# An FFT and token-mixing kernel: both DRAM bounces read back in pieces behind each write, and batch 1's first transform moved behind batch 0's last stage

## The chip, the cores and the metric

One core of a Trainium2 chip. The metric is the device time of one launch in microseconds (us), as the median of several runs. The kernel before took 667.63 us (3 runs, 667.39 to 667.77). PE is the tensor engine, which does the matmuls; ACT, DVE and POOL are the scalar, vector and GpSimd engines. SBUF is the core's own memory of 128 partitions (rows), which DMA, the transfer hardware with its 16 engines, reaches through ports. Each engine works through its instructions in order, and nearly all the transfers discussed here are issued, in order, by one queue (SP). The kernel holds its own scheduler: when it is built, it decides in which order each engine gets its instructions.

## The reference

Eight batches of 3072 rows by 256 columns. First a Fourier mixing layer, then a channel mix over neighbouring tokens:

```python
# x: (8, 3072, 256); w_r, w_i: (256, 256); w_k: (256, 1024); w_v: (1024, 256)
X = np.fft.rfft(x, axis=1)
Yr = X.real @ w_r - X.imag @ w_i + b_r
Yi = X.real @ w_i + X.imag @ w_r + b_i
Y  = shrink(Yr, 0.01) + 1j * shrink(Yi, 0.01)          # sign(v) * max(|v| - 0.01, 0)
y  = np.fft.irfft(Y, n=3072, axis=1)

prev = shift y by one token, zeros first               # (cut: written with np.concatenate)
k = np.maximum((mu_k * y + (1 - mu_k) * prev) @ w_k, 0)
v = (k * k) @ w_v
r = sigmoid((mu_r * y + (1 - mu_r) * prev) @ moe_w_r)
out = r * v
```

## The kernel before

The transform of 3072 points is split into 96 x 32, so a batch goes through three stages of matmuls. Between them, the index that lies on the partitions has to change, and this is done by writing a tile to DRAM and reading it back with the axes exchanged, a "bounce":

- `first` (8 matmul groups, L287): FFT over 96 points. It leaves tile A, 96 partitions, in four quarters of 8 columns each. Bounce A writes each quarter and reads the whole back as A2, 128 partitions.
- `middle` (L344 and on): FFT over 32 points, the layer's weights, and back. It leaves tile V in six pieces u = 0..5. Bounce V writes them and reads the whole back as V2, 96 partitions.
- `last` (8 groups, L489): the inverse over 96 points. Then the channel mix, called the token stage, in six tiles a batch (matmuls at L575, L600 and L617).

All three stages of batch b run beside the tokens of batch b - 1. The parts that the change touches:

```python
    r1_pool, ym_pool, v_pool, v2_pool = pool("r1p", 2), pool("ymp", 3), pool("vp", 3), pool("v2p", 4)
    ...
    READ_US, WRITE_US = 7.0, 5.0          # what the scheduler assumes of a read and of a write

    # first(b), for each quarter q of the columns
                def store(k):
                    nc.sync.dma_start(out=Adr[b][:, 8 * q:8 * q + 8, :], in_=a)          # 96 partitions, 384 KB
                    ...                                                                  # x loads of a later batch
                    if q == 3:
                        at(k + WRITE_US, fetch)

                def fetch(k):
                    A2[b] = a2_pool.tile([128, NG, D], BF16, name="A2")
                    for cj in range(4):                                                  # 4 reads of 32 partitions
                        nc.sync.dma_start(out=A2[b][32 * cj:32 * cj + 32],
                                          in_=Adr[b][24 * cj:24 * cj + 24].rearrange("g n d -> n g d"))
    ...
            needs = [("x", b, q), "FT"] + [("mid", 0)] * (b == 1)    # first(1) may follow middle(0)

    # middle(b), for each piece u
                def store(k):
                    for cj in range(4):                                                  # 4 writes of 32 partitions
                        nc.sync.dma_start(
                            out=Vdr[b][24 * cj + 4 * u:24 * cj + 4 * u + 4].rearrange("g n d -> n g d"),
                            in_=vt[32 * cj:32 * cj + 32])
                    if u == NU - 1:
                        at(k + WRITE_US, fetch)

                def fetch(k):
                    for q in range(4):
                        V2[b, q] = v2_pool.tile([96, 8, D], BF16, name="V2")
                    for q in (2, 3, 0, 1):                                               # 4 reads of 96 partitions
                        nc.sync.dma_start(out=V2[b, q], in_=Vdr[b][:, 8 * q:8 * q + 8, :])

    # the schedule
    START = 60.0
    ... first(b, *((45.0, 52.0) if b == 1 else (s - 0.9 * P, s - 0.1 * P)))
    ... last(b, 55.0, 60.0) if b == 0 else last(b, s + 0.75 * P, s + 0.95 * P)
```

An A read copies runs of 256 elements, 512 bytes, so it moves in packets of 512 bytes. A V2 partition is contiguous in DRAM; the whole-V reads move runs of 4 KB.

## Time and profile before

| | before |
|---|---|
| time | 667.63 us |
| PE idle, from the trace's records of PE | about 60 us, of which 45 before 93 us |
| batch 0: first middle matmul / first matmul of `last` / first token matmul | 31.9 / 76.4 / 85.8 us (each counted from its weight load; the prediction's 87.3 is the first token matmul itself) |
| period in the steady part, from one batch's first `last` matmul to the next's (batches 1 to 6) | 73 to 78 us |

The page's list of transfers (destination <- source, queue, count, size of one, median us from issue to landing) says that each read of the two bounces was a wide 384 KB one:

```profile
A<-Adr SPq DMA_DIRECT2D x32, 384.0 KB, 6.6
V<-Vdr SPq DMA_DIRECT2D x32, 384.0 KB, 6.2
```

### The profile page before, as it was taken

The page shows a single profiled execution, that of the slowest core. Times are in us where ns is not written, and L with a number is a line of the kernel's source. Part 1 is how long each engine was busy: PE and PEld are TensorE (multiplying, and loading weights), DVE is VectorE, ACT ScalarE, POOL GpSimd, SP SyncE. Part 2 cuts the span into 40 slices and gives each one's busy share as a digit, 9 for nine tenths or more (in the row PEclk, how much of TensorE's full clock was granted, in tenths as well). Part 3 has the DMA queues.
Part 4 walks back from the last instruction along what each step waited for, and adds up shares of the span by engine and source line. Part 5 has one row for each costly group of instructions (what it writes and reads, how often), then busy time and mean ns, then how long its engine had stood idle before and what let it go on. Part 6 is the DMA issues. An engine that isn't in the chain of part 4 may idle for free.

```text
span 662.8 us, 12033 instructions
## 1 busy us (share of the span) xinstructions
PE 593.6 (90%) x4722; PEld 435.5 (66%) x4801; DVE 483.8 (73%) x732; ACT 443.5 (67%) x469; POOL 25.2 (4%) x57
## 2 busy tenths in 40 slices
PE   4295379999999989998999989999999999999996
PEld 1273247777776767765777767766777777777764
DVE  5164368788778877797678787688677896788883
ACT  6254357767777767776577767778687767766662
POOL 5021000000000000000000000000000000000000
PEclk9689579999999999999999999999999999999999
DMA  8697996362247954488155874379233852362223
GB/s 182 119 189 166 290 213 121 79 183 65 57 112 175 230 128 111 103 227 197 33 128 128 237 146 96 88 202 207 86 104 104 223 113 68 78 183 56 65 72 88
DMA packets 75593, 90.33 MB, mean 136 GB/s; under 512 B 8976, under 2 KB 59920, under 8 KB 75536
## 3 DMA queue, kind: packets, MB, share of 16 engines
q1 hardware_dynamic: 69696, 75.53, 44.5%
q0 software_dynamic: 5840, 14.03, 12.5%
q8 instruction: 37, 0.61, 0.4%
q14 instruction: 20, 0.16, 0.1%
HBM read 53.22 MB, written 50.33 MB: 156 GB/s over the span
## 4 chain that ended last, share of the span: by engine, by line
PE 66%; DMA 17%; ACT 6%; DVE 5%; issue 3%; SPq 1%; POOL 0%; DVEq 0%; ACTq 0%; POOLq 0%
PE banks L617 22%; PE banks L575 19%; PE banks L394 11%; DMA Adr<-A 7%; DMA A<-Adr 6%; PE banks L600 4%; ACT rl L581 3%; PE banks L361 3%; PE banks L418 2%; PE banks L383 2%; ACT A L234 2%; PE banks L287 2%; DMA Vdr<-V 1%; DVE V L236 1%; PE banks L489 1%
## 5 line engine op out<-in xcount | busy, mean ns | idle before, releaser
L581 ACT ACTIVATE rl<-banks 128x1024 bf16<-128x1024 f32 x192 | 195.0, 1029 | 86.1 <-PE banks L575 73.2
L575 PE MATMUL banks<-xk,wk 128*128 128x512 bf16 x706 | 191.1, 383 | 4.0 <-DVE xk L553 1.4
L617 PE MATMUL banks<-wv,k 128*128 128x256 bf16 x1536 | 184.5, 274 | 0.4 <-DVE k L587 0.3
L587 DVE TENSOR_TENSOR k<-rl 128x1024 bf16<-128x1024 bf16 x192 | 131.8, 687 | 53.6 <-ACT rl L581 53.5
L617 PEld LDWEIGHTS <-k 128*128 128x128 bf16 x1536 | 150.3, 98 | 30.1 <-issue 1.8
L575 PEld LDWEIGHTS <-wk 128*128 128x128 bf16 x768 | 73.4, 98 | 57.9 <-issue 4.3
L394 PEld LDWEIGHTS <-XT 128*128 128x128 bf16 x768 | 75.4, 98 | 23.9 <-issue 0.8
L402 ACT ACTIVATE r<-banks,neglam 128x1024 bf16<-128x1024 f32 x48 | 53.4, 1113 | 40.6 <-PE banks L394 39.4
L406 DVE SCALAR_TENSOR_TENSOR Y<-banks,r 128x1024 bf16<-128x1024 f32 x48 | 58.5, 1222 | 28.1 <-ACT r L402 28.0
L394 PE MATMUL banks<-wr,XT 128*128 128x256 bf16 x384 | 73.8, 274 | 0.9
L394 PE MATMUL banks<-wi,XT 128*128 128x256 bf16 x384 | 73.8, 274 | 0.0
L553 DVE SCALAR_TENSOR_TENSOR xk<-diff,muk,YT 128x512 bf16<-128x512 bf16 x96 | 70.0, 746 | 0.6
L553 DVE SCALAR_TENSOR_TENSOR xr<-diff,mur,YT 128x512 bf16<-128x512 bf16 x96 | 69.2, 745 | 0.0
L624 DVE TENSOR_TENSOR o<-banks,rg 128x1024 f32<-128x1024 f32 x48 | 58.5, 1218 | 7.7 <-PE banks L617 7.7
L234 ACT ACTIVATE XT<-banks 128x1024 bf16<-128x1024 f32 (+2 forms) x39 | 37.8, 970 | 35.4 <-PE banks L361 23.5
L234 ACT ACTIVATE A<-banks 96x1024 bf16<-96x1024 f32 x49 | 49.2, 1020 | 17.6 <-DMA Adr<-A 12.0
L287 PE MATMUL banks<-xs,FT 96*96 96x512 bf16 x128 | 39.5, 420 | 19.0 <-ACT A L234 11.7
L600 PE MATMUL banks<-wrm,xr 128*128 128x256 bf16 x384 | 49.8, 272 | 3.5 <-ACT rl L581 2.2
L234 ACT ACTIVATE YT<-banks 128x768 bf16<-128x768 f32 x51 | 39.9, 815 | 16.2 <-PE banks L489 16.2
L605 ACT ACTIVATE rg<-banks 128x1024 bf16<-128x1024 f32 x48 | 49.2, 1026 | 1.9 <-PE banks L600 1.9
L600 PEld LDWEIGHTS <-xr 128*128 128x128 bf16 x384 | 37.1, 97 | 14.1 <-issue 3.8
L234 ACT ACTIVATE V<-banks 128x1024 bf16<-128x1024 f32 x33 | 33.8, 1023 | 9.9 <-PE banks L418 8.1
(91 smaller groups left out, 401.8 us busy)
## 6 DMA issues: line engine op xcount, KB each, us to landing
out_dram<-o SPq DMA_DIRECT2D x192, 128.0 KB, 2.2
xs<-in_x_dram POOLq DMA_DIRECT2D x32, 384.0 KB, 8.1
Adr<-A SPq DMA_DIRECT2D x32, 384.0 KB, 6.6
A<-Adr SPq DMA_DIRECT2D x32, 384.0 KB, 6.6
Vdr<-V SPq DMA_DIRECT2D x192, 64.0 KB, 1.8
V<-Vdr SPq DMA_DIRECT2D x32, 384.0 KB, 6.2
wk<-in_moe_w_k_dram POOLq DMA_DIRECT2D x1, 512.0 KB, 5.4
wv<-in_moe_w_v_dram POOLq DMA_DIRECT2D x1, 512.0 KB, 8.4
```

What stands on the lines that cost most here:

```text
L234: nc.scalar.activation(out, in_, AF.Copy, bias=0.0, scale=1.0)
L287: nc.tensor.matmul(ps[:96, 512 * i:512 * i + 512], FT, xt[:, 4 * p + 2 * i:4 * p + 2 * i + 2, :], start=True, stop=True)
L394: nc.tensor.matmul(o, lhs, w[:, c, :], start=False, stop=(w is wi and c == NCD - 1 and (i == 1 or not (u or half))))
L402: nc.scalar.activation(r1, ps, AF.Relu, bias=neglam, scale=1.0)
L406: nc.vector.scalar_tensor_tensor(out=y, in0=ps, scalar=LAM, in1=r1, op0=ALU.add, op1=ALU.min)
L553: nc.vector.scalar_tensor_tensor(out=m[:, c, :], in0=df[:, c, :], scalar=mu[:, c:c + 1], in1=yp[:, c, :], op0=ALU.mult, op1=ALU.add)
L575: nc.tensor.matmul(ps[:, 512 * f:512 * f + 512], wk[:, c, 128 * ff:128 * ff + 128], xk[:, c, :], start=(c == 0), stop=(c == NCD - 1))
L581: nc.scalar.activation(rl, ps, AF.Relu, bias=0.0, scale=1.0)
L587: nc.vector.tensor_tensor(out=k2, in0=rl, in1=rl, op=ALU.mult)
L600: nc.tensor.matmul(ps[:, 256 * q:256 * q + 256], xr[:, c, 128 * q:128 * q + 128], wrm[:, c, :], start=(c == 0), stop=(c == NCD - 1))
L617: nc.tensor.matmul(ps[:, 256 * q:256 * q + 256], K2[t][:, ff, 128 * q:128 * q + 128], wv[:, ff, :], start=(ff == 0), stop=(ff == NCF - 1))
L624: nc.vector.tensor_tensor(out=o.rearrange("p q d -> p (q d)"), in0=ps, in1=rg, op=ALU.mult)
```

## The change

Its intent: a read need not wait for the whole write. When a quarter of A, or a piece of V, has landed in DRAM, that part is read back at once, so that the read of the whole is nearly done when the last part is written. And batch 0's `last` stage no longer stands behind batch 1's `first`, so that tokens can begin earlier. Cut to its core:

```diff
-    ... v2_pool = ... pool("v2p", 4)
+    ... v2_pool = ... pool("v2p", 1)
-    READ_US, WRITE_US = 7.0, 5.0
+    READ_US, WRITE_US = 4.0, 4.0
@@ first(b), quarter q
+                    at(k + WRITE_US, fetch)
+
+                def fetch(k):
+                    if q == 0:
+                        A2[b] = a2_pool.tile([128, NG, D], BF16, name="A2")
+                    for cj in range(4):
+                        p0 = 32 * cj + 8 * q
+                        nc.sync.dma_start(out=A2[b][p0:p0 + 8],
+                                          in_=Adr[b][24 * cj:24 * cj + 24, 8 * q:8 * q + 8].rearrange("g n d -> n g d"))
                     if q == 3:
-                        at(k + WRITE_US, fetch)
-                def fetch(k):
-                    A2[b] = a2_pool.tile([128, NG, D], BF16, name="A2")
-                    for cj in range(4):
-                        nc.sync.dma_start(out=A2[b][32 * cj:32 * cj + 32],
-                                          in_=Adr[b][24 * cj:24 * cj + 24].rearrange("g n d -> n g d"))
-            needs = [("x", b, q), "FT"] + [("mid", 0)] * (b == 1)
-            if q == 3 and p == 1 and b >= 2:
+            needs = [("x", b, q), "FT"] + [("last", 0)] * (b == 1)
+            if q == 0 and p == 0 and b >= 2:
                 needs.append(("mid", b - 2))
@@ middle(b), piece u
+                    at(k + WRITE_US, fetch)
+
+                def fetch(k):
+                    if u == 0:
+                        V2[b] = v2_pool.tile([96, N2, D], BF16, name="V2")
+                    for cj in range(4):
+                        r0 = 24 * cj + 4 * u
+                        nc.sync.dma_start(out=V2[b][r0:r0 + 4], in_=Vdr[b][r0:r0 + 4])
-                    if u == NU - 1:
-                        at(k + WRITE_US, fetch)
-                def fetch(k):
-                    for q in range(4):
-                        V2[b, q] = v2_pool.tile([96, 8, D], BF16, name="V2")
-                    for q in (2, 3, 0, 1):
-                        nc.sync.dma_start(out=V2[b, q], in_=Vdr[b][:, 8 * q:8 * q + 8, :])
@@ (cut: the first use of the one V2 buffer waits for the last stage of the batch before)
@@ schedule
-    START = 60.0
+    START = 50.0
+            fc += last(b, 45.0, 50.0)                                            # b == 0
+            fb += first(b, START, START + 1.0) if b == 1 else first(b, s - 0.9 * P, s - 0.2 * P)
@@ (cut: the scheduler's assumed times for x, FT and the tables, by a few us)
```

So A is read in 16 pieces of 8 partitions, 96 KB each, and V in 24 pieces of 4 partitions, 64 KB each.

More of the change, by code (lines that the diff above doesn't have):

```diff
@@ L57 @@
     a_pool, a2_pool, xt_pool, xt0_pool = pool("ap", 3), pool("a2p", 2), pool("xtp", 3), pool("xt0p", 1)
-    r1_pool, ym_pool, v_pool, v2_pool = pool("r1p", 2), pool("ymp", 3), pool("vp", 3), pool("v2p", 4)
+    r1_pool, ym_pool, v_pool, v2_pool = pool("r1p", 2), pool("ymp", 3), pool("vp", 3), pool("v2p", 1)
     yt_pool, mx_pool, rl_pool, k2_pool = pool("ytp", 2), pool("mxp", 2), pool("rlp", 3), pool("k2p", 2)
@@ L211 @@
     heap, seq = [], itertools.count()
-    free = {"pe": 0.0, "act": 8.0, "dve": 14.0}
+    free = {"pe": 0.0, "act": 6.0, "dve": 13.3}
     done, slots = {}, {}
@@ L303, in store @@
                         done["x", n // 4, n % 4] = k + 9.0
-                    if q == 3:
-                        at(k + WRITE_US, fetch)
-                def fetch(k):
-                    A2[b] = a2_pool.tile([128, NG, D], BF16, name="A2")
-                    for cj in range(4):
-                        nc.sync.dma_start(out=A2[b][32 * cj:32 * cj + 32],
-                                          in_=Adr[b][24 * cj:24 * cj + 24].rearrange("g n d -> n g d"))
-                    done["A2", b] = k + READ_US
-                    if b == 0:
+                    at(k + WRITE_US, fetch)
[6 more added lines that the diff above has]
+                                          in_=Adr[b][24 * cj:24 * cj + 24, 8 * q:8 * q + 8].rearrange("g n d -> n g d"))
+                    if q == 3:
+                        done["A2", b] = k + READ_US
+                    if b == 0 and q == 3:
                         nc.gpsimd.tensor_copy(out=junk, in_=A2[0][:, 0, 0:1])
@@ L318, in fetch @@
                             load_x(1, n)
-                            done["x", 1, n] = k + 18.0
+                            done["x", 1, n] = k + 20.0
                 at(end, evac)
-            needs = [("x", b, q), "FT"] + [("mid", 0)] * (b == 1)
-            if q == 3 and p == 1 and b >= 2:
+            needs = [("x", b, q), "FT"] + [("last", 0)] * (b == 1)
+            if q == 0 and p == 0 and b >= 2:
                 needs.append(("mid", b - 2))
@@ L434, in store @@
                     done["v", b, u] = k + WRITE_US
-                    if u == NU - 1:
-                        at(k + WRITE_US, fetch)
-                def fetch(k):
-                    for q in range(4):
-                        V2[b, q] = v2_pool.tile([96, 8, D], BF16, name="V2")
-                    for q in (2, 3, 0, 1):
-                        nc.sync.dma_start(out=V2[b, q], in_=Vdr[b][:, 8 * q:8 * q + 8, :])
-                    done["V2", b] = k + READ_US
+                    at(k + WRITE_US, fetch)
[5 more added lines that the diff above has]
+                        nc.sync.dma_start(out=V2[b][r0:r0 + 4], in_=Vdr[b][r0:r0 + 4])
+                    if u == NU - 1:
+                        done["V2", b] = k + READ_US
                 if u == NU - 1:
@@ L464, in middle @@
                 needs = [("y", b, u), "GI"]
-                if u == NU - 1 and b >= 1:
+                if u == 0 and b >= 1:
                     needs.append(("last", b - 1))
@@ L488, in issue @@
                     for c in range(NCD):
-                        nc.tensor.matmul(pv[:, c, :, i, :], V2[b, n2 // 8][:, n2 % 8, 128 * c:128 * c + 128],
+                        nc.tensor.matmul(pv[:, c, :, i, :], V2[b][:, n2, 128 * c:128 * c + 128],
                                          FI, start=True, stop=True)
@@ L680 @@
         s = START + P * (b - 1)
-        fb += first(b, 0.0, 1.0) if b == 0 else first(b, *((45.0, 52.0) if b == 1 else (s - 0.9 * P, s - 0.1 * P)))
-        fa += middle(b, 20.0, 44.0) if b == 0 else middle(b, s, s + 0.5 * P)
-        fc += last(b, 55.0, 60.0) if b == 0 else last(b, s + 0.75 * P, s + 0.95 * P)
+        if b == 0:
+            fb += first(b, 0.0, 1.0)
+            fa += middle(b, 20.0, 44.0)
+            fc += last(b, 45.0, 50.0)
+        else:
+            fb += first(b, START, START + 1.0) if b == 1 else first(b, s - 0.9 * P, s - 0.2 * P)
+            fa += middle(b, s + (0.2 * P if b == 1 else 0.0), s + 0.5 * P)
+            fc += last(b, s + 0.75 * P, s + 0.95 * P)
     for t in range(NT):
@@ L700 @@
     for q in range(4):
-        done["x", 0, q] = 5.0 + 3.3 * q
-    done["FT"] = 8.0
-    at(13.3, tables)
+        done["x", 0, q] = 6.0 + 2.8 * q
+    done["FT"] = 5.0
+    at(16.0, tables)
     tab = [Unit(18.0, 0.1, ["FT"], table_fi)]
@@ L706 @@
     streams = [tok, val, fa, fb, fc, tab]
-    at(60.0 - 7.0, lambda k: mix_tokens(0, k))
+    at(START - 7.0, lambda k: mix_tokens(0, k))
     place, held, t = [0] * len(streams), {}, 0.0
```

## The prediction

> **What bounds the kernel now.** I read the page first (busy shares, slices, groups), then the chain of work that ended last, cut to 55 to 100 us, then the waits of PE, then the DMA view in short windows, because the change is about DMA.
>
> The page's busy line and slices, with the busy tenths of PE in 40 slices of 16.6 us:
>
> ```profile
> PE 593.6 (90%) x4722; PEld 435.5 (66%) x4801; DVE 483.8 (73%) x732; ACT 443.5 (67%) x469; POOL 25.2 (4%) x57
> PE   4295379999999989998999989999999999999996
> DMA  8697996362247954488155874379233852362223
> ```
>
> There are two regimes. From the seventh slice on PE is full, and DMA is about half used. Before that, about 93 us pass with PE half idle. The waits of PE say what the idle time is (columns: waited us, times, longest):
>
> ```profile
> PE banks L344 <- DMA A<-Adr: 23.5, 5, 12.4
> PE banks L287 <- ACT A L234: 11.7, 1, 11.7
> PE banks L287 <- DMA xs<-in_x_dram: 7.0, 2, 6.0
> PE banks L489 <- DMA V<-Vdr: 3.6, 4, 1.6
> ```
>
> L344 is the first matmul of the middle stage, which waits for the whole A bounce to be read back. 12.4 us of it belong to batch 0 at 19.5 to 32 us, 3.4 to batch 1 and the rest to later batches: in the window from 93 us on, the same wait is 7.7 us in 3 times, so the steady stage loses little. The chain shows the second stretch:
>
> ```profile
> 60.30 11.49 DMA Adr<-A
> 71.91 1.23 DVE A L236
> 73.20 8.43 DMA Adr<-A
> 83.54 8.54 DMA A<-Adr
> 93.37 1.71 PE banks L575 x4
> ```
>
> Batch 1's first transform stands on PE and on the DMA queue ahead of batch 0's last stage. Its A writes and the four x loads for later batches hold the DMA engines from 58 to 72 us, batch 0's V is asked for only at 71.2 us, and the token stage starts in earnest at 93 us.
>
> **What the Trainium skill says.** (1) DMA: Bandwidth & Descriptors, section "Why a DMA increments its semaphore by 16 and not by 1": a DMA runs on k engines, k being the largest number up to 16 that divides the slowest dimension of both access patterns, and on this queue the lowest-numbered k. The kernel before has 32 or 96 partitions outermost everywhere, so k is 16. The change makes it 8 for A reads (8 partitions by 24 by 256) and 4 for V reads (4 by 8192). No run so far shows a small k.
> (2) SBUF — State Buffer, section "Door 1: The DMA port swizzle": partitions 0..3 are one port (27.6 GB/s measured), 0..31 eight ports (189 GB/s measured). The trace before agrees. While only A reads into 32 partitions run, the DMA view gives, in 28.4 to 30.2 us,
>
> ```profile
> DMA packets 628, 0.32 MB, mean 177 GB/s; under 512 B 7, under 2 KB 628, under 8 KB 628
> q1 hardware_dynamic: 628, 0.32, 120.8%
> ```
>
> that is 22 GB/s per port. It is no limit of the engines: where V writes to DRAM were queued up (51 to 51.6 us) the same 512 B packets ran at
>
> ```profile
> DMA packets 428, 0.20 MB, mean 329 GB/s; under 512 B 50, under 2 KB 427, under 8 KB 428
> ```
>
> and in 26.6 to 27.4 us, where the reads pass from partitions 32..63 to 64..95, the mean rises to 211 GB/s and falls back.
> (3) Same page, section "Can I just issue two DMAs to hit both halves?": two such DMAs on different partitions gained 6%, as they follow each other on the same engines. Here there is one counter-example: eight out stores of 32 partitions, piled up behind an A read, ran at 402 GB/s at 236 to 237 us, so engines that are out of step can use different ports.
>
> **The change part by part.**
> *Order at the start.* last(0) is put directly behind middle(0), first(1) behind it. PE's order agrees: the 24 matmuls of L287 between the last L418 and the first L489 of batch 0 are gone. It removes the DMA stretch 60 to 84 us from the path of batch 0. If reads were as fast as hoped, tokens would begin about 7 us after V has landed (before: last piece 79.9, first token matmul 87.3), with V landing some 3 us after the last evacuation at about 56: 66 us in place of 92. PE has then done 5 us less work (first(1) and the start of the tokens), so the gain is 92 - 66 - 5 = 21 us. The three steady waits, 7.7 us, go too if the last quarter's read is short. A write and a read after the move of first(1) stand only 9 us of PE work before middle(1), which may give back 6 us. Sum at full speed: about -20 us.
> *A reads in 16 pieces instead of 4.* 1.57 MB a batch, now 98 KB each on 8 engines and 2 ports. At 22 GB/s per port 98 KB take 2.2 us; 16 of them 36 us a batch, if they follow one another; the four of one quarter use two pairs of ports. Before, the four took 8.8 us. Without a port limit: 329/16 = 20.6 GB/s per engine, 1.57 MB / 8 / 20.6 = 10 us.
> *V reads in 24 pieces instead of 4.* 64 KB each on 4 engines and one port: 2.4 us at 27 GB/s, 58 us a batch in a row. Without a port limit 402/16 = 25 GB/s per engine and 16 us.
> *Issues.* 96 + 160 more of them at 0.4 to 0.5 us (V reads 376 ns, A reads 518 ns median) on a queue with 480 before: about 110 us of the queue's time, spread over 560; no bound. The queue now waits for a write to land ahead of each group of reads, with stores behind it; o and V have 2 and 3 buffers, which covers some 6 to 12 us.
> *What engines 0 to 3 carry per batch.* Before: 44.5% + 12.5% of 662.8 us over 8 batches = 47 us on each engine. Take off the old A reads (8.8 us at 120% = 10.6) and V reads (1.57 MB at about 260 GB/s = 6): 30 us stay. Add the new reads:
> - in a row through the ports: 58 + 36 + 30 = 124 us
> - half out of step (each group of four V reads in 6.5 us instead of 9.6, each A quarter in 6.5 instead of 9; my guess): 39 + 26 + 30 = 95 us
> - ports no limit: 16 + 10 + 30 = 56 us
> A batch has 75 to 77 us on PE now (the chain's A writes of successive batches start at 217.2, 293.1, 370.9). So in the first two cases four DMA engines become the bound, and every DMA, which ends only when its slowest engine does, queues behind them.
>
> **The rivals.**
> *Hope of the change:* reads are hidden behind writes and the start shrinks. For it: DMA is half used, and the path is as the chain says. It gives 667.6 - 20 = about 647 us. It needs engines 0 to 3 to stay under 75 us a batch.
> *Narrow reads, fully in a row:* for it the 177 GB/s and the skill's one port. Startup: A of batch 0 read from 14 to about 50, V by about 112; then 7 batches of 124 overlapped a little, and 55 us of last tokens: about 980 us.
> *Narrow reads, partly out of step:* an engine that gets ahead finds the next port free and runs away from the others, as the out stores did. A of batch 0 by 42, V by about 95, seven times about 92 = 644, and 55 for the last stage and tokens: about 795 us.
> *A draw:* engines 0 to 3 stay just under the period, and late reads for batch 1 eat the gain: 665 us.
>
> **Range and chances.** I give the hope 20%, the draw 8%, the partly stepped case 45% and the full row 27%. The median of that is near 795 us; 8 in 10 lie between 645 and 980. Faster by over 2% needs the skill's k or the port limit to be of no account here: 0.20. Within 2%: 0.08. Slower: 0.72.
>
> **What would show it right or wrong.** Right: while V reads run, the mean rate falls to 25 to 100 GB/s with 4 engines' worth of packets; V<-Vdr takes over 5 us from issue to landing although it is 64 KB; PE gets long waits at L346 (A reads) and L492 (V reads) in every batch; the busy share of PE falls to 75% or less and tokens begin later than 93 us in spite of the new order. Wrong: 64 KB V reads land in some 2.5 us, the four reads of an A quarter in under 5, PE stays full from about 67 us, and waits at L346 vanish. Then the start's order decides and I have missed by the whole DMA term. If the A reads are slow but V reads fast, the loss is in first-to-middle alone, under 60 us of load, and the time is near the draw.

## More of the kernel before

On the page, the granted clock of the tensor engine in 40 slices (9 is 90% or more of full speed) is low only in the first slices, and the packets of the whole run are counted by size:

```profile
PEclk9689579999999999999999999999999999999999
DMA packets 75593, 90.33 MB, mean 136 GB/s; under 512 B 8976, under 2 KB 59920, under 8 KB 75536
```

One row of the table of windows is a steady batch (columns: window, its length, then busy us and, in brackets, instructions of PE, PE weight load, DVE, ACT, POOL, then the granted clock, the DMA share and GB/s). PE is busy 71.86 of 76 us at full clock, so the steady part is bound by PE:

```profile
236.00:312.00 76.00, 71.86 (x587) 53.23 (x597) 59.43 (x86) 53.86 (x57) 2.03 (x4) 1.00 0.60 147
```

## The result and the profile after

The changed kernel took 912.83 us (median of 4 runs, 900.48 to 914.2), with a correct result. Two of its runs count as fast (911.55 and 900.48); against the fast runs of the kernel before it is 1.356 times as long, with a 95% interval of 1.342 to 1.371. Ratios here and below are the mean time of one kernel's fast runs over that of the other's of the same rounds, so they are not quite the ratio of the medians that I quote.

The page's busy line and slices of the kernel after, to lay beside those in the prediction and above. One slice is now 22.7 us:

```profile
PE 615.3 (68%) x4801; PEld 443.3 (49%) x4801; DVE 489.5 (54%) x737; ACT 437.6 (48%) x464; POOL 25.3 (3%) x57
PE   4090725951999239990699608994399908994997
PEclk9995876975999659995799958998599958997999
DMA  8693566555346654565536646356444546243222
```

PE was full from the seventh slice on; now a gap returns at every batch (the digits 0 to 3 in the PE line), and the clock line falls to 0.5 to 0.7 at the same places. PE is busy for 22 us more than before although it does the same matmuls: after each gap it runs for a while at half the clock. (A part of the 22 is that the trace of before lacks 79 matmul records, 4722 in place of 4801.) The waits of PE (us in total, times, longest) name the gaps:

```profile
PE banks L492 <- DMA out_dram<-o: 160.2, 6, 33.3
PE banks L492 <- DMA V<-Vdr: 49.8, 2, 28.0
PE banks L346 <- DMA Adr<-A: 26.8, 1, 26.8
PE banks L346 <- DMA A<-Adr: 24.7, 1, 24.7
```

L492 is the first matmul of `last` and L346 that of `middle`. There are 8 waits for V, one a batch, 210 us in all, and two for A, in batches 0 and 1, 51.5 us. The name `out_dram<-o` on six of the V waits is wrong, and it is worth seeing how one notices. The matmul reads V2, not `o`; and the trace's packet records show that the last 16 KB packet of a V landed at 92.5 us (batch 0) and 332.7 us (batch 2), and PE went on at 93.1 and 334.1. The list of transfers gives the reason for the wrong name:

```profile
A<-Adr SPq DMA_DIRECT2D x128, 96.0 KB
V<-Vdr SPq DMA_DIRECT2D x192, 64.0 KB
```

The landing times are gone. They are counted from 16 completions of a DMA, and these DMAs no longer post 16. The packet counts show what they post. Before, 480 DMAs of the SP queue with 16 completion packets of 4 bytes each, and 576 packets of 4 bytes of the four small loads of `mu` on the same queue, made 8256 of 4 bytes. After, if an A read runs on 8 engines and a V read on 4, there should be 416 x 16 + 128 x 8 + 192 x 4 + 576 = 9024, which is 768 more; with 16 for all it would be 4096 more. The page says 9744 small packets in place of 8976, and that is 768:

```profile
DMA packets 74058, 90.34 MB, mean 99 GB/s; under 512 B 9744, under 2 KB 60688, under 8 KB 73232
```

So the skill's k (the prediction's first citation) is what this chip does: 8 engines and 4. That they are the lowest-numbered ones, no record here shows.

How fast do the narrow reads run? Two DMA windows with nothing but A reads, and nothing but V reads:

```profile
DMA packets 422, 0.23 MB, mean 57 GB/s; under 512 B 20, under 2 KB 416, under 8 KB 422
q1 hardware_dynamic: 422, 0.23, 65.8%
```

```profile
DMA packets 49, 0.38 MB, mean 63 GB/s; under 512 B 26, under 2 KB 26, under 8 KB 26
q1 hardware_dynamic: 49, 0.38, 20.6%
```

The first is 26 to 30 us, the second 86 to 92 us. A reads, 177 GB/s before, now pass at 57. The last column is the time that packets took, as a share of 16 engines: 0.658 x 16 x 4 us / 422 = 100 ns for a packet of 512 bytes, where the window in the prediction gives 1.208 x 16 x 1.8 us / 628 = 55 ns. In single microseconds of it the rate is 49, 69, 49 and 61 GB/s; 49 comes back often where only A reads run (at 33, 36, 37 and 40 us too), and I take it for two ports' worth, and the higher values for reads of two port pairs that overlap. A 16 KB packet of V takes 1.26 us on average over the whole run.

On the queue, the waits for writes have grown. For the A reads (L311) and the V reads (L444), us in total, times, longest:

```profile
SPq L311 <- DMA Adr<-A: 94.6, 24, 11.7
SPq L444 <- DMA Vdr<-V: 62.4, 19, 8.2
```

The queue also waits for the narrow reads themselves. These are its V writes (L433) and out stores (L636), which need nothing of what is being read:

```profile
SPq L433 <- DMA V<-Vdr: 51.3, 39, 3.8
SPq L636 <- DMA V<-Vdr: 35.4, 31, 2.1
SPq L636 <- DMA A<-Adr: 31.4, 29, 1.7
```

The waits in the trace say why. The SP transfers of this program take eight semaphores in turn, and one that takes a semaphore over waits until the transfer that had it before, eight issues earlier, has landed. So no more than eight are under way, and a slow read holds up whatever comes eight issues behind it. All its waits for reads to land are 180 us here and 8 us before.

Finally two windows: 71 to 93 us, in which PE does 0.29 us of work while batch 0's V is on its way, and a steady batch, to compare with the one of before:

```profile
71.00:93.00 22.00, 0.29 (x3) 0.01 (x1) 0.00 (x0) 1.25 (x2) 0.00 (x0) 0.53 0.34 96
241.00:351.00 110.00, 75.59 (x603) 54.78 (x601) 59.92 (x87) 54.14 (x58) 2.03 (x4) 0.84 0.55 101
```

A batch takes 100 to 110 us instead of 73 to 78 (batches 1 to 6, as above; from batch 0 to 1 it is 130), at two thirds of the DMA rate. Batch 0 is late too: first middle matmul 46.2 us (31.9 before), first `last` matmul 93.1 (76.4), first token matmul 101.5 (85.8), in spite of the new order. In the whole run PE stands idle for about 288 us instead of 60. That is 228 of the 247 us between the two profiled spans (909.8 and 662.8); the slow clock is what can make up the other 19 or so. TensorE: Matmul & The Clock Gate in the Trainium skill, section "Part 1: The HAM clock gate", puts the drop to half clock at one idle window of about 3.4 us; here, in the gap from 300.7 to 334.1 us, the granted clock fell to 0.5 at 304.3, 3.6 us after PE stopped, and came back at 338.4, 4.4 us after it went on. The trace agrees.

### The profile page after: what moved, and what is told of

The parts are those of the page before. It is cut to its first block, busy times and chain, and to the rows that moved or that the text cites. A ratio compares the mean times of both kernels' runs of the same rounds, so it can differ in the third digit from the quotient of the medians.

```text
span 909.8 us, 12428 instructions
## 1 busy us (share of the span) xinstructions
PE 615.3 (68%) x4801; PEld 443.3 (49%) x4801; DVE 489.5 (54%) x737; ACT 437.6 (48%) x464; POOL 25.3 (3%) x57
## 2 busy tenths in 40 slices
DMA packets 74058, 90.34 MB, mean 99 GB/s; under 512 B 9744, under 2 KB 60688, under 8 KB 73232
## 4 chain that ended last, share of the span: by engine, by line
DMA 48%; PE 38%; SPq 6%; ACT 3%; issue 2%; DVE 1%; POOL 0%; ACTq 0%; POOLq 0%; DVEq 0%
DMA V<-Vdr 14%; PE banks L620 13%; DMA Vdr<-V 12%; DMA A<-Adr 11%; PE banks L578 10%; DMA Adr<-A 6%; PE banks L396 5%; DMA out_dram<-o 4%; SPq L444 3%; PE banks L492 3%; SPq L311 3%; PE banks L603 2%; PE banks L363 2%; ACT rl L584 1%; PE banks L287 1%
## 5 line engine op out<-in xcount | busy, mean ns | idle before, releaser
L578 PE MATMUL banks<-xk,wk 128*128 128x512 bf16 x768 | 199.2, 385 | 5.2 <-ACT V L234 1.7
L620 PE MATMUL banks<-wv,k 128*128 128x256 bf16 x1536 | 194.7, 283 | 0.6 <-DVE k L590 0.3
L492 PE MATMUL banks<-FI,V 96*128 96x96 f16 x512 | 34.1, 222 | 211.1 <-DMA out_dram<-o 160.2
L620 PEld LDWEIGHTS <-k 128*128 128x128 bf16 x1536 | 154.9, 101 | 35.9 <-issue 1.8
L492 PEld LDWEIGHTS <-V 96*128 96x128 bf16 x512 | 30.3, 107 | 220.5 <-issue 184.1
L506 DVE COPY YT<-YT 128x576 bf16<-128x576 bf16 x16 | 4.9, 308 | 178.7 <-ACT YT L234 178.7
L234 ACT ACTIVATE A<-banks 96x1024 bf16<-96x1024 f32 x45 | 45.1, 1018 | 12.5 <-PE banks L287 10.7
```

What stands on the lines that cost most here:

```text
L234: nc.scalar.activation(out, in_, AF.Copy, bias=0.0, scale=1.0)
L492: nc.tensor.matmul(pv[:, c, :, i, :], V2[b][:, n2, 128 * c:128 * c + 128], FI, start=True, stop=True)
L578: nc.tensor.matmul(ps[:, 512 * f:512 * f + 512], wk[:, c, 128 * ff:128 * ff + 128], xk[:, c, :], start=(c == 0), stop=(c == NCD - 1))
L620: nc.tensor.matmul(ps[:, 256 * q:256 * q + 256], K2[t][:, ff, 128 * q:128 * q + 128], wv[:, ff, :], start=(ff == 0), stop=(ff == NCF - 1))
```

## The experiments

Four things changed at once: the order at the start, the A pieces, the V pieces, and with the pieces the width of a read. My theory was the prediction's: narrow reads, on few SBUF ports and few DMA engines, are the loss. Against it, in the expectations, stand the new order itself and the pieces as such: more issues on the in-order queue, and reads that wait there for writes, whatever their width (rival 3). All results were correct. All edits are against the changed kernel unless said otherwise. Kernels share the runs of the kernel before: 668.86 us (the first four), 666.94 (e5 to e8), 669.40 (e9 to e12).

| run | A read | V read | order | us | ratio to before |
|---|---|---|---|---|---|
| before | 4 x 32 partitions | whole, 4 x 96 | old | 667.63 | 1 |
| after | 16 x 8 | 24 x 4 | new | 912.83 | 1.356 |
| e1_order_only | 4 x 32 | whole | new | 674.67 | 1.008 |
| e2_a_pieces | 16 x 8 | whole | new | 753.42 | 1.127 |
| e3_v_pieces | 4 x 32 | 24 x 4 | new | 753.37 | 1.125 |
| e4_v_rows16 | 4 x 32 | 6 x 16 | new | 662.87 | 0.990 |
| e5_v_spread | 4 x 32 | 24 x 4, 4 apart | new | 707.84 | 1.061 |
| e6_v_late | 4 x 32 | 24 x 4, all at the end | new | 792.86 | 1.189 |
| e7_a_half | 8 x 16 | whole | new | 699.52 | 1.046 |
| e8_x_late | 4 x 32 | 6 x 16 | new, x(1) late | 660.05 | 0.989 |
| e9_a_spread | 16 x 8, 4 apart | whole | new | 694.71 | 1.037 |
| e10_both_wide | 16 x 8, 4 apart | 6 x 16 | new | 692.02 | 1.033 |
| e11_both_wide_old_order | 16 x 8, 4 apart | 6 x 16 | old | 720.49 | 1.079 |
| e12_v_rows_old_order | 4 x 32 | 6 x 16 | old | 682.77 | 1.020 |

By the 2% that counts as the same, e1, e4 and e8 are the same as the kernel before, e12 is unclear, and all the others are slower. "New order" stands for the whole new schedule: the due times of the stages in every batch moved with it.

### e1_order_only: the new order with both reads whole

```diff
-                    at(k + WRITE_US, fetch)            # A after every quarter, V after every piece
+                    if q == 3:  (V: if u == NU - 1:)
+                        at(k + 5.0, fetch)             # 4 reads of 32 (V: of 96) partitions, as before; READ_US 7
-    pool("v2p", 1)
+    pool("v2p", 4)
```

> The changed order alone: both reads whole as in the kernel before (four A reads of 32 partitions, four V reads of 96), everything else as in the changed kernel. Theory 1 (the narrow reads are the loss: 8 and 4 partitions wide, so on few DMA engines and few SBUF ports): 640 to 652 us, the 20 us gain that my prediction gave the order. Rival 2 (the new order of batch 0 and 1, or the schedule's new constants, is what stalls PE): 800 us or more. A draw with the kernel before (660 to 672) would mean that the order's gain is eaten by batch 1's shorter way from first to middle.

Measured 674.67 us (673.53 to 676.57), ratio 1.008 (1.005 to 1.012). The order costs little, but its gain of 20 us did not come, so my expectation was a miss. The chain of work that ended last, from 50 to 110 us (start, us, what), shows why:

```profile
62.16 6.75 DMA V<-Vdr
...
76.14 6.95 DMA Adr<-A
...
84.49 5.08 DMA Adr<-A
...
91.77 10.20 DMA A<-Adr
```

V of batch 0 lands at 68.9 us, and the first token matmul comes at 76.4 instead of 85.8 us: 9 us earlier, not the 26 that I had set in the prediction. But batch 1's `first` now stands on PE at 73 to 81 us instead of 56 to 60, so its A is read back only at 102 us (before, 92). PE's idle time up to 100 us is 41 us against 45. The wait has moved from batch 0's V to batch 1's A. That takes the gain back: batch 1's first `last` matmul comes at 146.3 us, 147.1 before. The loss comes later: batch 3's comes at 302.9 us, 293.9 before, and from there on the distance stays at 9 to 12. What costs these 9 us, no run here shows.

### e2_a_pieces and e3_v_pieces: one bounce in pieces at a time

```diff
# e2: only A in pieces                              # e3: only V in pieces
-  V: at(k + WRITE_US, fetch), 24 reads of 4        -  A: at(k + WRITE_US, fetch), 16 reads of 8
+  V: whole, behind the last write, as in e1        +  A: whole, behind the last write, as in e1
```

> The changed kernel with the V reads whole again; the A reads stay in 16 pieces of 8 partitions. Theory 1: the low DMA engines carry some 30 us of other DMAs, 6 of V and 26 to 36 of A in a batch, 62 to 72 us, just under PE's 75: the steady stage holds, only the start is late (the A read of batch 0 landed some 14 us later than before), so 655 to 690 us. Rival 3 (waits for each write inside the DMA queue hold up what stands behind them): 700 to 800, as the A pieces wait longest (95 us of the queue's waits in the changed kernel, against 62 for V).

> The changed kernel with the A reads whole again; the V reads stay in 24 pieces of 4 partitions. Theory 1: low engines carry 30 + 11 + 39 to 58 us in a batch, over PE's 75, so most of the loss is here: 750 to 850 us, with a PE wait of 10 to 30 us ahead of the last stage of every batch. Rival 3 (the queue's waits): no more than 720, as the V writes land in 2 us and wait less.

Measured: e2 753.42 us (750.55 to 759.88), e3 753.37 us (751.22 to 755.08), each some 79 us more than e1 on the same chip. e3 came as expected. e2 did not: I had thought A's pieces nearly harmless by themselves (655 to 690), and they cost as much as V's. The time lies in the range that I had given to rival 3, the waits in the queue (700 to 800); e9 below takes the two apart for A.

The two gaps look different. In e3 PE waits at the last stage in every batch, 22 us in batch 0 and then 6 to 16. In e2 its waits at the middle stage are long only at the start, 21.5 us in batch 0 and 28.5 in batch 1, with 1 to 4 us at A and up to 6 at V in each later batch. The waits of PE in e2 at the first matmul of `middle`:

```profile
PE banks L346 <- DMA A<-Adr: 61.6, 6, 28.5
```

The next quarter's write stands on the queue behind the last quarter's slow reads, and the next reads behind that write: the queue waited 98.8 us in e2 for A writes to land (23 times, 11.6 at most). In all it waited 97 us for narrow reads to land in e2 and 99 in e3, where it is 17 in e1.

Both at once, in the changed kernel, cost more than the sum: its fast runs average 906 us, 231 above e1, where 79 + 79 is 158. About 74 us come from the two together.

### e4_v_rows16: V in pieces, but each piece one read of 16 partitions

The rows of V in DRAM and on the partitions of V2 are put in another order (piece u first), so that the four narrow reads of a piece become one read of 16 neighbouring partitions. The order of FI's rows, with which V2 is multiplied, follows. Bytes and writes stay as in e3, and a read still waits for the writes of its piece; the reads are 6 instead of 24.

```diff
# A whole as in e1, and:
-                            out=Vdr[b][24 * cj + 4 * u:24 * cj + 4 * u + 4].rearrange("g n d -> n g d"),
+                            out=Vdr[b][16 * u + 4 * cj:16 * u + 4 * cj + 4].rearrange("g n d -> n g d"),
-                    for cj in range(4):
-                        r0 = 24 * cj + 4 * u
-                        nc.sync.dma_start(out=V2[b][r0:r0 + 4], in_=Vdr[b][r0:r0 + 4])
+                    nc.sync.dma_start(out=V2[b][16 * u:16 * u + 16], in_=Vdr[b][16 * u:16 * u + 16])
```

> A reads whole; V pieces kept, one behind each write, but the rows of V stand in DRAM and SBUF in the order of the pieces, so that a piece is one read of 16 partitions (256 KB, 16 rows outermost) in place of four of 4. The waits for writes in the DMA queue stay. Theory 1: 16 engines and 4 ports, 256 KB in 2.5 to 3 us, 15 to 18 us a batch: no stall, 635 to 655 us. Rival 3 (waits in the queue): as slow as the run with V pieces of 4 partitions, within 5%.

Measured 662.87 us (659.8 to 666.74), ratio 0.990 (0.985 to 0.995), 8 us above the range that I gave and far from rival 3's. V is still read in pieces behind each write, and the whole loss of e3 is gone. The queue's waits for V writes ahead of the reads are not: 53.0 us in all, 51.8 in e3. What is gone is its waiting for reads to land, 4 us instead of 99. The slices of PE and its waits at the last stage (L493 here):

```profile
PE   4291787987999999999999999999999999999996
PE banks L493 <- DMA V<-Vdr: 14.1, 1, 14.1
```

One wait for V in batch 0, a gap of 5.4 us at the same line in batch 1, and no steady gap at all. So reading V in pieces behind each write costs nothing, once each read is 16 partitions wide, on 16 engines and four ports. As this also takes 18 of 24 issues away, the next two runs keep all 24. The longest remaining wait of PE is at the start: the first V writes take 7 to 9 us behind batch 1's x loads, and V lands at 70 us.

### e5_v_spread: the same 4 engines, but 4 ports

The four partitions of a narrow read are put 4 apart, so that they lie on four ports instead of one; the outermost size is still 4, so the DMA stays on 4 engines.

```diff
# e3 and:
-  nc.sync.dma_start(out=V2[b][r0:r0 + 4], in_=Vdr[b][r0:r0 + 4])
+  nc.sync.dma_start(out=V2[b][16 * u + cj:16 * u + cj + 13:4], in_=Vdr[b][r0:r0 + 4])
```

> As the run with V pieces of 4 partitions (A whole; 753 us), still 24 reads of 64 KB with 4 rows outermost, so still 4 DMA engines, but the four partitions of a read lie 4 apart (16u+cj, +4, +8, +12), so they are on four SBUF ports instead of one; the rows of the inverse table are permuted to match. If the port is the limit (theory 1a): a row runs at its engine's 25 GB/s, 16 KB in 0.65 us instead of 1.08, and the stall ahead of the last stage goes: 655 to 680 us. If the number of engines is the limit (theory 1b): 735 to 765, no change.

Measured 707.84 us (704.39 to 712.74), ratio 1.061 (1.056 to 1.066): between the two expectations. Of e3's 12.5% over the kernel before, about half is gone with the port. The 16 KB packets took 778 ns on average instead of 1080 in e3. The queue's waits for reads to land fell from 99 us to 12. What stays is the 4 engines and the queue, which I couldn't part: a spread read takes 0.56 us to issue, where a plain one takes 0.25 to 0.32.

### e6_v_late: the same narrow reads without their waits for writes

All 24 narrow reads are issued in a row behind the last write, as the whole reads were.

```diff
# e3 and:
-                    at(k + WRITE_US, fetch)                   # after each piece
+                    if u == NU - 1:
+                        at(k + WRITE_US, fetch)               # 24 reads, no wait between them
```

> A whole; the 24 narrow V reads are kept but all issued after the batch's last write, so the DMA queue no longer waits for a write between the pieces. Theory 1 (narrow reads are slow in themselves): now none of their time is hidden, 24 rows of 1.08 us per engine are 26 us behind the last write, with 14 us of PE work to cover them: a longer stall per batch, 780 to 850 us. Rival 3 (the waits in the queue are the loss): the waits are gone, 660 to 690 us.

Measured 792.86 us (790.31 to 795.71), ratio 1.189 (1.184 to 1.194). Taking the waits for writes away makes it worse. As the run also takes away the stage behind which the reads could hide, that alone doesn't clear these waits; e4, which keeps them and loses nothing, does. PE waits 12 to 19 us for V in each later batch (108.5 us in seven, with the same wrong name as above) and 25.6 in batch 0:

```profile
PE banks L490 <- DMA out_dram<-o: 108.5, 7, 19.4
PE banks L490 <- DMA V<-Vdr: 25.6, 1, 25.6
```

This run also measures the port by itself. By the packet records, the 24 reads of a batch took 17 to 23 us from the first packet's start to the last landing, 1.57 MB in about 20 us: 79 GB/s. If four engines always stood at one port, it would take 58 us at the 27 GB/s that the prediction takes from the skill. The median packet took 619 ns, 26 GB/s on each engine. So in a long row the four engines must get out of step and use more ports than one. What then limits is in part open: their number allows about 106 GB/s at that packet time, and the queue stands still for 79 us in this run (128 times) until a V read eight issues ahead has landed.

### e7_a_half: A in 8 reads of 16 partitions

Two quarters of A are read together, so a read covers 16 partitions: 16 engines, 4 ports.

```diff
# e2 (V whole) and:
-                    for cj in range(4):                       # after every quarter, 8 partitions
+                    if q % 2: ...                             # after every second quarter
+                        p0, n0 = 32 * cj + 8 * (q - 1), 8 * (q - 1)
+                        nc.sync.dma_start(out=A2[b][p0:p0 + 16],
+                                          in_=Adr[b][24 * cj:24 * cj + 24, n0:n0 + 16].rearrange("g n d -> n g d"))
```

> V whole; A read back in halves behind every second write, 8 reads of 16 partitions in a batch (16 engines, 4 ports) in place of 16 reads of 8 partitions (8 engines, 2 ports; 753 us). Theory 1: 196 KB at 4 x 22 GB/s are 2.2 us, so 18 us a batch on 16 engines, 54 us of load with the rest: no overload, 668 to 695 us. Rival 3 (waits in the queue): half as many waits, so about half of that run's loss stays, 700 to 725 us.

Measured 699.52 us (692.38 to 700.93), ratio 1.046 (1.040 to 1.052), between the two. The half reads run at about 100 GB/s, four ports. PE waits 14.1 us for A in batch 0 and 17.4 in batch 1. The last quarter's write, issued at 92.7 us, landed only at 105.7, behind the reads of the first half.

### e8_x_late: e4, with batch 1's x loads behind batch 0's V

```diff
# e4 and: the four load_x(1, n) move from the end of A's fetch(0) to the end of V's fetch(0),
#         behind a small GpSimd copy that reads V2[0]
```

> The run with V pieces of 16 rows (663 us) with batch 1's x loads held back until batch 0's V has been read. In that run the first two groups of V writes took 6 to 9 us each, because the loads of x for batch 1, asked for at 35 us and not needed before 75, fill the DMA engines until 51 us. If that is what keeps batch 0's V until 70 us: V lands at about 61 to 63, tokens begin 6 to 9 us earlier, and the time is 652 to 658 us. If the V stage is paced by PE, ACT and the queue's own issues instead, or the held-back loads delay batch 1 by as much: 660 to 668.

Measured 660.05 us (657.38 to 662.66), ratio 0.989 (0.985 to 0.993), within the second of the two ranges. The first eight V writes of batch 0 now land in 1.6 to 1.8 us, the others in 2.6 to 4.6, and V at 65.8 us, but batch 1's `first` then waits for its x until 73.3 us. It is the fastest version that I found, by its ratio level with e4: 1.1% under the kernel before, inside the 2% that counts as the same.

### e9_a_spread: A's pieces on 8 ports, still 8 engines

The 8 partitions of an A piece are put 4 apart. The tables' row order and the order in which `last` takes its columns follow.

```diff
# e2 (V whole) and:
-                        p0 = 32 * cj + 8 * q
-                        nc.sync.dma_start(out=A2[b][p0:p0 + 8],
+                        p0 = 32 * cj + q
+                        nc.sync.dma_start(out=A2[b][p0:p0 + 29:4],
```

> V whole; A in the same 16 pieces of 8 partitions behind each write as in the run that took 753 us, still 8 rows outermost, so still 8 DMA engines, but the 8 partitions of a piece lie 4 apart, so they are on 8 SBUF ports instead of 2 (the tables are built for the permuted partitions, 4 more tiny DVE instructions at the start). If the ports are A's limit (theory 1a): the 512 B packets go back from 85-100 ns to 50 or less, 98 KB in some 0.7 us, and the time comes down to that of the run with the order alone or below, 660 to 680 us. If the number of engines (1b) or the waits in the queue (rival 3) are: 730 to 760.

Measured 694.71 us (692.34 to 696.48), ratio 1.037 (1.033 to 1.042), where e2 had 1.127 with the same number of reads, engines and waits for writes. It lies between the two ranges that I gave. A DMA window with A reads alone, 94 to 96 us, to compare with the 57 GB/s of the kernel after:

```profile
DMA packets 689, 0.34 MB, mean 169 GB/s; under 512 B 28, under 2 KB 689, under 8 KB 689
q1 hardware_dynamic: 689, 0.34, 58.0%
```

0.580 x 16 x 2 us / 689 = 27 ns a packet instead of 100, at three times the rate, on the same 8 engines. For most of A's loss it was the ports: three quarters of the loss over e1 come back on the same 8 engines, and the queue's waits for reads to land fall from 97 us to 14. The rest, about 20 us, I put on the queue, which no run shows by itself: the 16 spread reads take 0.66 to 0.69 us each to issue (0.3 to 0.5 for the whole ones), and the queue still waits 67.8 us for A writes (24 times), with stores and V's transfers behind it.

### e10, e11 and e12: wide in both, and the old order

```diff
# e10: e9's A and e4's V together
# e11: e10 with the old order:   [("last", 0)] -> [("mid", 0)],  START 50 -> 60,  and the due times of before
# e12: e4 with the old order, the same edit
```

> Both bounces in pieces, as the change meant it, and none of them on few ports: A pieces spread over 8 ports, V pieces as one read of 16 rows, new order. If width is all that was wrong with the change, it now beats the kernel before: A of batch 0 read some 4 us earlier than whole, no waits for A later on, 645 to 658 us. If the order's loss at batch 1 stays as it is: 655 to 663.

> The same pieces with the order of the kernel before (batch 1's first transform right behind batch 0's middle stage, and its start constant of the schedule). If the new order gains nothing, as the run with the order alone said (675 against 669), this is the faster of the two: 645 to 655 us. If the new order pays once the reads are quick: 660 or more.

> V pieces of 16 rows, A whole, old order. Against the run with the new order (663 us) it tells the order apart once more: if the order costs about 1%, 653 to 660 us; if it gains, 668 or more.

Measured: e10 692.02 us (689.36 to 694.78), e11 720.49 (718.73 to 728.84), e12 682.77 (681.21 to 686.0; ratio 1.020, 1.016 to 1.024). e10 was a miss, slower than both of its ranges. e11 and e12 fell on the side where the new order pays (660 or more, 668 or more), and e11 far out. e10 is no better than e9: with A in 16 pieces, 3% are lost even with the ports out of the way. PE waits 14.1 us for V in batch 0, 11.9 for A in batch 1, and 2 to 9 us at the last stage in batches 1 to 5. In e11 batch 0's last V read is issued at 74.87 us (66.70 in e10), sixteen A reads of batch 1 follow it on the queue at 0.66 to 0.69 us each from 75.35 to 91.3 us, and PE waits 17.9 us for batch 0's V, 10.2 for batch 1's A and 4 to 11 us at the last stage in batches 2 to 6.

e12 against e4 measures the order again. They were run at other times. With V in wide pieces the new order is worth 3% (0.990 against 1.020), with both in pieces 4% (e10 against e11), while with whole reads e1 shows it to cost 0.8%. In e12 the last V writes of batch 0 took 10 us, beside batch 1's A and x, and PE waited 16.2 us for V; but e4's wait there is 14.1, so this crowd is not where the 3% are. At batch 1's first `last` matmul e12 is even ahead, 145.0 us against 153.1; at batch 7's it is behind, 607.8 against 591.3, as a batch between 2 and 6 takes 74 to 81 us there and 73.5 in e4. So what the new schedule gains here it gains in the steady part, perhaps by its due times and not by the order of batches 0 and 1; no run parts the two.

## Why the prediction was right or wrong

The call (slower, at 0.72) was right, and so was the mechanism: narrow reads on few ports and engines. The time lay in the range, but 795 was short of the 913 measured. The case of 795 was a sum of three: 95 us to batch 0's V, seven batches of 92 (644), and 55 for the last stage and tokens. Measured from PE's first `last` matmul of batch 0 and of batch 7, these are 93, 744 and 73 (the last was 70 before the change, so 55 was too low from the start). That 913 still lay inside is owed to the case of 980, whose 58 us a batch for V didn't come; that is luck.

- **k and the ports: right, and shown.** The count of completion packets gives 8 and 4 engines. e4 against e3 (0.990 against 1.125) keeps V in pieces but makes them wide, and V's whole loss goes; e5 keeps all 24 reads and, with more ports alone, gets half of it back. e9 against e2 (1.037 against 1.127) takes only the port limit away, and three quarters of A's loss goes.
- **A, "36 us a batch, if they follow one another", or 26 half out of step: between.** At the 57 GB/s that the window of A reads has on average, a batch's 1.57 MB take 28 us, at the 49 GB/s of its slow microseconds 32.
- **V, "58 us a batch in a row", or 39 half out of step: too high.** 24 packets on each of four engines at 1.26 us are 30 us, and e6 showed about 20 when they run by themselves. So one port's rate didn't bind a row of such reads: 63 GB/s in the window above, 79 in e6.
- **"Four DMA engines become the bound": not quite.** With the measured terms, 30 (V) + 28 to 32 (A) + the old 30 make 88 to 92 us, an estimate as the records don't name the engine of a packet. The prediction had 95, and took that sum, or 92 for the steady batches, as the period. The period is 100 to 110 us. The step that failed is that a batch takes no longer than its most loaded engines. What it left out is the in-order queue: a slow read holds back the transfer eight issues behind it (180 us of such waits in all, 8 before), a write issued late lands late behind the reads, and the next reads wait for it (94.6 us for A, 62.4 for V). The first of these goes with the loss: 97 and 99 us in e2 and e3, 4 in e4, though e5 still loses 6% at 12. The waits for writes alone don't: e4 has 53.0 us of them for V and loses nothing. No run changes how many transfers may be under way, so the share of each stays open. "Issues ... no bound" was thus wrong in that the cost of an issue and the wait ahead of it are paid in order, ahead of transfers that PE needs.
- **The interaction.** e2 and e3 alone lose 79 us each, together about 74 more than the sum. By the terms above, the lowest engines would carry at most 32 + 6 + 30 = 68 us a batch in e2 and 30 + 10.6 + 30 = 71 in e3, both under PE's 75, and 88 to 92 with both, over it. That fits, but no run tested it alone; and as both stay under 75 by this estimate, it leaves the 79 us of each to the queue's waits.
- **The order at the start, "gain 21 us" and "sum about -20": wrong.** e1 gave +0.8%. Tokens began at 76.4 us, not 66, as V landed at 68.9 us and not at about 59 (its reads were issued at 61 and took 8 us); and the give-back, put at 6 us, was all of the gain by batch 1, since its A came 10 us later; another 9 us went between batches 1 and 3.
- **What it said to look for.** V at 25 to 100 GB/s (63), waits at L492 in every batch, PE's share at 75% or less (68%) and tokens later than 93 us (101.5) all came. Waits at L346 in every batch did not: they were in batches 0 and 1 alone, perhaps because the gaps at V hide the later A reads; no run tests that. And "V<-Vdr takes over 5 us to landing" can't be read off, as the page has no landing times for such DMAs.
- **The slow clock** was not in the prediction. It is worth at most the 19 us that PE's idle time leaves over.

Open: how the rest of e5, and the 3% of e9 and e10, divide between the time of issues, the waits for writes and the limit of eight under way; and why the new schedule helps with V in wide pieces and not with whole reads. The best version, e4 or e8, gains 1%, as the steady part was full on PE before: bounces read in pieces had only the start to win.

## What to carry to other kernels

Before cutting a transfer into pieces, look at what a piece becomes: how many partitions, thus ports, it covers, and what its outermost size divides by; if a piece gets narrow, change the layout until it is one read of 16 or more partitions, which here turned +12.5% into -1%. Pieces are also more transfers on an in-order queue, each with a wait for its write, and a slow one holds back what is issued behind it: with A that cost 3% even with the ports out of the way, with V's wide pieces nothing. So use pieces only where the whole read is on the path, and look at what the queue itself waits for. And a reordering that lets one batch go first takes its gain from the next one: follow both before counting it.

## What the Trainium skill lacked or had wrong

- SBUF — State Buffer, "Can I just issue two DMAs to hit both halves?": the +6% that the page measured for two concurrent DMAs is not general. 24 narrow reads in a row (e6), each of 4 partitions on one port and each on another port than the one before it, ran at about 79 GB/s in all, three times the 27.6 GB/s of the page's one-port row, with a median packet of 619 ns; so reads on different ports do overlap there.
- Same page, "Door 1: The DMA port swizzle": its measured rows are for single transfers of 1 MiB. Packets of 512 bytes on 2 ports ran at 49 GB/s, and on 4 ports at about 100, which is about 25 a port, near its 27.2; on the 8 ports of 32 partitions 177 GB/s before. It lacks the remedy that e9 shows: the same 8 partitions taken 4 apart went from 57 to 169 GB/s.
- DMA: Bandwidth & Descriptors, "Why a DMA increments its semaphore by 16 and not by 1": right (768 more completion packets, as k = 8 and 4 give). No page says what it does to a profile: the transfers with k under 16 have no landing time there, and 160.2 us of waits for V carry the name of the out stores.
- No page that I read has the cost of issuing a read with strided partitions: 0.56 us for 4 partitions and 0.66 to 0.69 us for 8, where the plain narrow ones took about 0.3 us and the whole A reads 0.5.
- No page that I read says that a program's queue may stand still because its eight DMA semaphores are all in use: 180 us of such waits for reads in the kernel after, 8 in the kernel before.
